# The bound for the softmax: squares kept as a maximum over the blocks, and the shift's rows sent by DMA

## The chip, the cores and the metric

The kernel runs on one core of a Trainium2 chip. The core has a matrix engine (TensorE, PE in the profile, its weight loads PEld), a vector engine (VectorE, DVE), a scalar engine (ScalarE, ACT), GpSimd (POOL), a queue for transfers (SyncE, SP) and 16 DMA engines that all queues share. The metric is the device time of one execution in microseconds (us), lower is better. It is given as the median of several runs, and one more execution is recorded by the profiler.

## The reference

One input x of 2048 tokens with 512 features is normalised. From it come an attention with 32 heads of 16 features and a gated network with 1792 hidden features; the product of the two is added to x.

```python
xn = _layernorm(x)                                    # (1, 2048, 512)
q, k, v = (xn @ wqkv) split into 32 heads of 16
scores = einsum("bhqd,bhkd->bhqk", q, k) * 16 ** -0.5
o = einsum("bhqk,bhkd->bhqd", softmax(scores), v)
s = o.reshape(1, 2048, 512) @ wo
g = silu((silu(xn @ w_gate) * (xn @ w_up)) @ w_down)
return x + s * g
```

All inputs are fp32. The softmax is over all 2048 keys, with no mask.

## The kernel before, in words

The work is written out by hand: each engine runs its instructions in the order in which the code issues them, and waits where its operands are not ready. Products in fp32 are split into a high and a low part (fp32r), so that a projection of one tile takes 12 products: 4 chunks of the 512 features, 3 terms each.

**The first stage** is the pool block `pro` (lines 446 to 797). It goes over 4 blocks of 512 tokens. A block has 12 slots: 8 feature tiles (`feature_tile`, 128 features of queries for m below 4, of keys above) and 4 value tiles (`value_tile`, 128 tokens each). Block 0 does its value tiles first, the others last. While block b is projected, the x of block b + 1 is loaded, its statistics are taken (`stats`, `rates`: L533 to L549), its tiles are normalised (`norm`, L553, VectorE) and transposed on TensorE (`turn_x`, L556), and the transposed tile is split into its high part (ScalarE, L565) and its low part (VectorE, L568). `rates` comes in slot 5, the first `norm` in slot 6, the first transpose in slot 7.

A feature tile is 12 products into a PSUM tile (four of these rotate), then ScalarE writes the squares in bf16 (`sq`, L637) and the high part (L638), VectorE the low part (`parts`, L639), and SP sends both parts to DRAM (L641). GpSimd makes the low parts of the weights (L497) and sends the transposed x and the values to DRAM.

**The shift.** Softmax is taken without a maximum of its own for each query. A common bound serves all queries: half of the largest sum of squares of a query and of a key, times 1.02, which no product of the two passes. For that the squares of each block are summed over the 16 features of a head on TensorE (`squares`, L595, a product with the indicator `ind`), 8 products for each block, put into the two PSUM banks `bankx` and `banky`. `flush` issues them (for block 0 behind the first tile of block 1, for the others in slot 8) and takes the maximum of each bank (L683). Before the last value tiles, the maxima are joined: over partitions by a transpose (`tops`, L745, L746), scaled by 0.51 (L747), and compared with 160 (`flag`, L748). If the flag were 0, the general path in `tc.If` (L765) would find a maximum for each query. The shift goes into the score products as two more rows of the queries (`qst`; the matching rows of `kst` are ones): its high and its low part, the low one 0 here. Two small products (`sel`, `selq`, L754 and L755) put the number on the partitions that need it, ScalarE copies it into `shift` and into the first `qst` (L756, L759), and GpSimd stores `shift` to the DRAM tensor `sh_d` in four parts (L761). From there each later set of queries gets its rows (`load_shift`, L113).

**In slot 9 of the last block** a first hidden feature of the gated network is computed between value tiles (`fill`, L174 for its products; `split_gu` L134 and L135 for its weights, `load_gu` L127 for a later feature's).

**The second stage** goes over 32 units (8 groups of 4 heads, 4 query blocks). Each unit has 8 steps: 8 score products (L835), 4 exponentials on ScalarE (L837), 16 value products (L356), and between them shares of the gated network (`ffn`, L174) by a fixed plan. Its tiles take the SBUF space of the first stage, so some of its first instructions wait until the last transfers of that stage have read their source.

Of the kernel before, what the change touches and what calls it, by code (L numbers as in the profile page):

```python
# [9 lines left out]
F32 = mybir.dt.float32  # L10
F32R = mybir.dt.float32r
BF = mybir.dt.bfloat16
I32 = mybir.dt.int32
AF = mybir.ActivationFunctionType
ALU = mybir.AluOpType
# [35 lines left out]
def tile_block(ctx: ExitStack, tc: tile.TileContext, x, wqkv, wo, w_gate, w_up, w_down, out):  # L51
# [394 lines left out]
    with ExitStack() as pro:  # L446
        pc = pro.enter_context(tc.tile_pool(name="pc", bufs=1))
        p2 = pro.enter_context(tc.tile_pool(name="p2", bufs=2))
        p3 = pro.enter_context(tc.tile_pool(name="p3", bufs=4))
        p5 = pro.enter_context(tc.tile_pool(name="p5", bufs=9))  # L450
        plast = pro.enter_context(tc.tile_pool(name="plast", bufs=1))
        pps = pro.enter_context(tc.tile_pool(name="pps", bufs=4, space=PSUM))

# [55 lines left out]
        dve.memset(ind, 0.0)  # L509
        dve.reduce_sum(indf, ident.rearrange("p (h d) -> p h d", d=DH), axis=AX.X)  # L510
        dve.tensor_copy(ind[:, :8], indf)
        sel = plast.tile([1, 2 * NG * NB], F32, name="sel")
        selq = plast.tile([1, HALF + 2], F32, name="selq")
        row = plast.tile([1, 512], F32, name="row")
        dve.memset(sel, 0.0)
        dve.memset(selq, 0.0)
        dve.memset(row, 1.0)
        peak = pc.tile([P, 2, NB], F32, name="peak")
        vt = plast.tile([P, NG, NT, VW], F32, name="vt")
        vt5 = vt.rearrange("p g t (h d) -> p g t h d", h=4)  # L520
        for t in range(NT):
# [103 lines left out]

        s4 = pc.tile([1, 1], F32, name="s4")
        flag = const.tile([1, 1], I32, name="flag")
        pk = pc.tile([P, 2], F32, name="pk")
        sm = pc.tile([P, 1], F32, name="sm")
        shift = plast.tile([2 * NG * NB, 512], F32R, name="shift")  # L630

        def feature_tile(b, m):
            xh, xl = xt[b % 2]
            ps = project([(wh[:, m, c], wl[:, m, c], c) for c in range(DT)], xh, xl, None)
            parts = p3.tile([P, 2, TB], F32R, tag="parts", name="parts")
            sq = p5.tile([P, TB], BF, tag="sq", name="sq")
            act(sq, ps, AF.Square)  # L637
            nc.scalar.copy(parts[:, 0], ps)  # L638
            dve.tensor_sub(parts[:, 1], ps, parts[:, 0].bitcast(F32))  # L639
            dst = (q_d if m < 4 else k_d)[:, (m % 4) * P:(m % 4 + 1) * P, b * TB:(b + 1) * TB]  # L640
            sp.dma_start(dst.rearrange("s f t -> f s t"), parts.bitcast(F32))  # L641
            return m, sq

        def value_tile(b, t):
            xh, xl = xt[b % 2]
# [21 lines left out]
        def copy_fx(i):  # L667
# [2 lines left out]
            j, h = divmod(i, 2)  # L670
            dst = fx[halves[h], j].rearrange("p (c u) t -> u p c t", u=2)[u]
            nc.scalar.copy(dst[:, 2 * w:2 * w + 2], xt[0][j][halves[u], 2 * w:2 * w + 2])

        pend = []

        def add():
            while pend:
                squares(*pend.pop(0))

        def flush(b):  # L680
            add()
            for j in range(2):
                dve.reduce_max(peak[:, j, b:b + 1], banks[j], axis=AX.X)  # L683

        for b in range(NB):
            more = b + 1 < NB
# [2 lines left out]
            for n, (make, i) in enumerate(slots):  # L689
                if b == 0:  # L690
                    if n + 5 < 12:
                        load_w(worder[n + 5])
                    if n >= 2 and n + 2 < 12:
                        high_w(worder[n + 2])
                        low_w(worder[n + 2])
                if n == (1 if b else 2) and more:
                    load_x(b + 1)
                if b == 2 and n in (6, 7):
                    load_gu(n - 6)
                if b == 2 and n == 8:  # L700
                    load_wd(0)
                if not more and n == 2:
                    split_gu(0)
                    for bank in acc:
                        dve.memset(bank, 0.0)
                if not more and n in (1, 3):
                    load_k(0, n // 2)
                if not more and n == 5:
                    load_q(0)
                if not more and n == 6:  # L710
                    for c in range(2):
                        load_v(0, c)
                if b == 0 and n == 1:
                    norm(2)
                    norm(3)
                made = make(b, i)
                if b == 0 and n == 2:
                    split_x(0, 0, xf)
                if b < 2 and 0 <= 12 * b + n - 3 < 16:
                    copy_fx(12 * b + n - 3)  # L720
                if n == 0 and b == 1:
                    flush(0)
                if make is feature_tile:
                    pend.append(made)
                if b == 0 and n == 11:
                    ring(0, 2, one)
                    queries(0, one)
                if more:
                    for t in range(NT):
                        if n == 2 + (t if b else t // 2):  # L730
                            stats(t)
                    if n == (5 if b else 4):
                        rates(0, NT)
                    if 6 <= n < 10:
                        norm(n - 6)
                    if 7 <= n < 11:
                        turn_x(b + 1, n - 7)
                if n == 8 and b:
                    flush(b)
                if not more and n == 8:  # L740
                    dve.reduce_max(pk, peak, axis=AX.X)
                    dve.tensor_add(sm, pk[:, 0:1], pk[:, 1:2])
                if not more and n == 9:
                    tops = pps.tile([P, 512], F32, tag="ps", name="tops")
                    nc.tensor.transpose(tops[0:1, :P], sm, ident)  # L745
                    dve.reduce_max(s4, tops[0:1, :P], axis=AX.X)  # L746
                    dve.tensor_scalar(s4, s4, 0.51, None, op0=ALU.mult)  # L747
                    dve.tensor_scalar(flag, s4, LIMIT, None, op0=ALU.is_le)  # L748
                    dve.tensor_scalar(sel[:, :NG * NB], row[:, :NG * NB], s4, None, op0=ALU.mult)
                    for h in range(2):  # L750
                        dve.tensor_copy(selq[:, h * HALF:h * HALF + 1], s4)
                    fill(3 * DC)
                    low, high = [pps.tile([P, 512], F32, tag="ps", name="low") for _ in range(2)]
                    mm(high[:2 * NG * NB, :8], sel, row[:, :8], start=True, stop=True, skip_group_check=True)  # L754
                    mm(low[:HALF + 2, :8], selq, row[:, :8], start=True, stop=True, skip_group_check=True)  # L755
                    act(shift, high[:2 * NG * NB, 0:1].to_broadcast([2 * NG * NB, 512]), AF.Copy, scale=-1.0)  # L756
                    for h in range(2):
                        two_rows = slice(h * HALF, h * HALF + 2)
                        act(qst[0][two_rows], low[two_rows, None, 0:1].to_broadcast([2, 2, 512]), AF.Copy, scale=-1.0)  # L759
                    for j in range(4):  # L760
                        pool.dma_start(sh_d[:, j * 512:(j + 1) * 512], shift.bitcast(F32))  # L761
                    fast = nc.values_load(flag, min_val=0, max_val=1)


# [177 lines left out]
```

## Time and profile before

| | us |
|---|---|
| median of 3 runs | 1436.54 |
| lowest and highest | 1436.37, 1437.82 |
| profiled execution | 1437.19 |
| its span | 1435.4 |

| engine | busy us | share of the span |
|---|---|---|
| TensorE | 1428.2 | 99% |
| ScalarE | 1112.2 | 77% |
| VectorE | 535.0 | 37% |
| GpSimd | 89.6 | 6% |

In the profile's rows `out<-in` names the tiles of the program, L12 is a line of the kernel, and x is how many instructions are in the row. In a timeline the first column is the start in us, the second the duration, and a bracket gives the idle time in front and what ended it. Products are pipelined, so the distance between two starts tells what one costs in sequence, and its duration doesn't. Rows of groups end with the busy time, the mean of one in ns, and the idle time of the engine in front of them.

The first stage lasts until about 161 us of the span, when the first score is computed.

### The profile page before, as it was taken

Reading aid. Unit: us, or ns where it says so; the run is one execution under the profiler, and the core shown is the slowest. Engines: PE = TensorE matmul, PEld = TensorE weight load, DVE = VectorE, ACT = ScalarE, POOL = GpSimd, SP = SyncE. Lnnn points to the kernel's source line nnn. Section 1 sums busy time; section 2 is a strip of 40 time slices with the busy share of each in tenths; the row PEclk is TensorE's granted clock in tenths of the full one; section 3 lists DMA queues with packets and bytes.
Section 4 is the critical chain, followed back from the end, with each engine's and each line's share of the span. In section 5 each row is a group of like instructions: output and inputs, shape, how many; then the busy total and the mean of one; then the engine's idle time right before and its main releaser. Section 6 shows DMA issues by size and latency. Waiting matters only on the chain.

```text
span 1435.4 us, 26786 instructions
## 1 busy us (share of the span) xinstructions
PE 1428.2 (99%) x11221; PEld 803.6 (56%) x11221; DVE 535.0 (37%) x886; ACT 1112.2 (77%) x1236; POOL 89.6 (6%) x103
## 2 busy tenths in 40 slices
PE   9999999999999999999999999999999999999998
PEld 7778655555555555555555555555555555555555
DVE  5543344112523342134323431243344422243665
ACT  6733688888888888788888888888888887888764
POOL 4200200000000000000000000000000000000154
PEclk9999999999999999999999999999999999999999
DMA  7778652032274321142553320342824210412552
GB/s 222 264 242 253 157 119 64 17 96 60 64 153 119 97 65 34 38 105 71 111 134 90 94 49 12 79 104 58 177 79 121 65 42 12 101 30 78 196 183 104
DMA packets 127668, 149.15 MB, mean 104 GB/s; under 512 B 12604, under 2 KB 79676, under 8 KB 126772
## 3 DMA queue, kind: packets, MB, share of 16 engines
q1 hardware_dynamic: 122196, 126.71, 34.5%
q0 software_dynamic: 4912, 20.12, 3.8%
q8 instruction: 91, 1.49, 0.5%
q10 hardware_dynamic: 432, 0.52, 0.1%
q14 instruction: 37, 0.30, 0.1%
HBM read 107.20 MB, written 40.11 MB: 103 GB/s over the span
## 4 chain that ended last, share of the span: by engine, by line
PE 88%; DVE 0%; issue 0%; DVEq 0%
PE acc L356 33%; PE bankx L174 32%; PE score L835 20%; PE banky L174 3%; DVE y L889 0%; PE acc L882 0%; DVE y L895 0%; PE score L882 0%; PE banky L882 0%; DVEq L938 0%; DVE rl L886 0%; DVEq L895 0%
## 5 line engine op out<-in xcount | busy, mean ns | idle before, releaser
L837 ACT ACTIVATE pr<-score 128x1024 f32<-128x1024 f32 x1024 | 993.2, 1023 | 223.0 <-PE score L835 222.4
L356 PE MATMUL acc<-pr,vst 128*17 128x512 f32 x4096 | 489.2, 595 | 0.0
L835 PE MATMUL score<-qst,kst 50*128 50x512 f32 x2048 | 352.1, 421 | 0.0
L835 PEld LDWEIGHTS score<-qst,kst 50*128 50x128 f32 x2048 | 177.1, 184 | 263.7 <-ACT pr L837 225.7
L174 PE MATMUL bankx<-fx,guh 64*128 64x512 f32 x896 | 288.8, 392 | 0.1
L174 PE MATMUL banky<-fx,guh 64*128 64x512 f32 x896 | 288.8, 392 | 0.0
L356 PEld LDWEIGHTS acc<-pr,vst 128*17 128x17 f32 x4096 | 94.0, 96 | 234.6 <-issue 233.8
L204 DVE SCALAR_TENSOR_TENSOR ga<-th,bankx 128x512 f32<-128x512 f32 x56 | 38.5, 688 | 445.3 <-ACT th L203 445.3
L174 PEld LDWEIGHTS bankx<-fx,guh 64*128 64x128 f32 x896 | 165.7, 185 | 34.5 <-issue 0.9
L174 PE MATMUL banky<-fx,gul 64*128 64x512 f32 x448 | 175.3, 391 | 0.0
L174 PE MATMUL bankx<-fx,gul 64*128 64x512 f32 x448 | 175.3, 391 | 0.0
L174 PEld LDWEIGHTS banky<-fx,guh 64*128 64x128 f32 x896 | 165.7, 185 | 2.8
L174 PE MATMUL banky<-wd,hh 64*128 64x512 f32 x672 | 166.7, 389 | 0.0
L174 PE MATMUL bankx<-wd,hh 64*128 64x512 f32 x672 | 166.6, 389 | 0.0
L174 PEld LDWEIGHTS bankx<-wd,hh 64*128 64x128 f32 x672 | 124.0, 185 | 26.1
L174 PEld LDWEIGHTS banky<-wd,hh 64*128 64x128 f32 x672 | 124.0, 185 | 1.4
L174 PEld LDWEIGHTS bankx<-fx,gul 64*128 64x128 f32 x448 | 82.9, 185 | 17.8
L174 PEld LDWEIGHTS banky<-fx,gul 64*128 64x128 f32 x448 | 82.8, 185 | 1.4
L588 PE MATMUL ps<-xt,wh 128*128 128x512 f32 x256 | 80.9, 397 | 0.1
L222 DVE COPY facc<-bankx 128x512 f32<-128x512 f32 x16 | 11.1, 692 | 171.1 <-PE banky L174 150.3
L135 DVE TENSOR_TENSOR gul<-gur,guh 128x1024 fp32r<-128x1024 f32 x56 | 68.6, 1225 | 2.1
L588 PEld LDWEIGHTS ps<-xt,wh 128*128 128x128 f32 x256 | 47.8, 188 | 11.8 <-DVE xt L568 0.5
(161 smaller groups left out, 1019.1 us busy)
## 6 DMA issues: line engine op xcount, KB each, us to landing
gur<-in_B_w_gate_dram SPq DMA_DIRECT2D x56, 256.0 KB
gur<-in_B_w_up_dram SPq DMA_DIRECT2D x56, 256.0 KB
wdr<-in_B_w_down_dram SPq DMA_DIRECT2D x56, 256.0 KB
kst<-k_d SPq DMA_DIRECT2D x192, 64.0 KB
qst<-q_d SPq DMA_DIRECT2D x192, 64.0 KB
fx<-xt_d SPq DMA_DIRECT2D x24, 512.0 KB
q_d<-parts SPq DMA_DIRECT2D x16, 512.0 KB
k_d<-parts SPq DMA_DIRECT2D x16, 512.0 KB
```

What stands on the lines that cost most here:

```text
L135: dve.tensor_sub(lo, raw, hi.bitcast(F32))
L174: mm(bank, lhs[h], rhs[h], start=start, stop=stop)
L204: dve.scalar_tensor_tensor(ga, th, 1.0, bankx, op0=ALU.add, op1=ALU.mult)
L222: dve.tensor_copy(facc[:, t], bankx)
L356: mm(a[h * 32:h * 32 + DH + 1], v[:, kt % CT, h * (DH + 1):(h + 1) * (DH + 1)], probs[2 * i + h // 2][:, h % 2], start=kt == 0, stop=kt == ...
L588: mm(ps, w, a[:, c], start=n == 0, stop=n == 3 * DT - 1)
L835: mm(score[j][:, h], k[r, j, kc * P:(kc + 1) * P], q[r, j], start=True, stop=True)
L837: exps.append(act(pr, score[j], AF.Exp, scale=0.25))
```

## The change

Squares of block 0 are written straight into eight tiles `top`, one for each feature tile. In the later blocks they go into one of two rotating `sq` tiles (nine before), and VectorE takes the maximum of `top` and `sq` into `top`. The sums over the features of a head are made once, of the eight `top` tiles, in slot 8 of the last block; the two maxima over the banks are taken there, and added. The bound is thereby that of the largest squares at the same place in a block, not of one token; on the reference's inputs it rises from 69 to 99 by its formula.

The shift's row is made on one partition by VectorE (0 plus the number, times -1, 512 columns). SP copies it into the first row of each half of `qst`, and GpSimd stores it to the upper half of `sh_d`, which is read as 128 rows of 512, by one DMA whose source is that one row each time. The rows of the low part, which are 0, are no longer sent with it: GpSimd writes the lower half of `sh_d` at the start from a row of zeros, and clears the two rows in each half of `qst` at the end of block 0. The products L754 and L755, the tiles `sel`, `selq` and `pk`, and the three ScalarE copies are gone.

```diff
-        p5 = pro.enter_context(tc.tile_pool(name="p5", bufs=9))
+        p5 = pro.enter_context(tc.tile_pool(name="p5", bufs=2))
...
-        sel = plast.tile([1, 2 * NG * NB], F32, name="sel")
-        selq = plast.tile([1, HALF + 2], F32, name="selq")
         row = plast.tile([1, 512], F32, name="row")
-        dve.memset(sel, 0.0)
-        dve.memset(selq, 0.0)
-        dve.memset(row, 1.0)
-        peak = pc.tile([P, 2, NB], F32, name="peak")
+        dve.memset(row, 0.0)
+        peak = pc.tile([P, 2], F32, name="peak")
+        top = [pc.tile([P, TB], BF, name=f"top{m}") for m in range(8)]
...
-        shift = plast.tile([2 * NG * NB, 512], F32R, name="shift")
+        shift = plast.tile([1, 512], F32R, name="shift")
+        none = sh_d[NG * NB:].rearrange("u (j t) -> (u j) t", t=512)
+        pool.dma_start(none, row[:, None].to_broadcast([1, NG * NB * 4, 512]))
...
-            sq = p5.tile([P, TB], BF, tag="sq", name="sq")
+            sq = p5.tile([P, TB], BF, tag="sq", name="sq") if b else top[m]
...
-            return m, sq
+            if b:
+                dve.tensor_max(top[m], top[m], sq)
...
-        def flush(b):
-            add()
-            for j in range(2):
-                dve.reduce_max(peak[:, j, b:b + 1], banks[j], axis=AX.X)
...
+                if not more and n == 8:
+
+                    for m in range(8):
+                        squares(m, top[m])
+                    for j in range(2):
+                        dve.reduce_max(peak[:, j:j + 1], banks[j], axis=AX.X)
+                    dve.tensor_add(sm, peak[:, 0:1], peak[:, 1:2])
...
-                if n == 0 and b == 1:
-                    flush(0)
-                if make is feature_tile:
-                    pend.append(made)
                 if b == 0 and n == 11:
                     ring(0, 2, one)
                     queries(0, one)
+                    for h in range(2):
+                        pool.memset(qst[0][h * HALF:h * HALF + 2].bitcast(F32), 0.0)
...
-                    dve.tensor_scalar(sel[:, :NG * NB], row[:, :NG * NB], s4, None, op0=ALU.mult)
+                    dve.tensor_scalar(shift, row, s4, -1.0, op0=ALU.add, op1=ALU.mult)
                     for h in range(2):
-                        dve.tensor_copy(selq[:, h * HALF:h * HALF + 1], s4)
+                        sp.dma_start(qst[0][h * HALF:h * HALF + 1].bitcast(F32), shift.bitcast(F32)[:, None].to_broadcast([1, 2, 512]))
+                    pool.dma_start(sh_d[:NG * NB].rearrange("u (j t) -> (u j) t", t=512),
+                                   shift.bitcast(F32)[:, None].to_broadcast([1, NG * NB * 4, 512]))
                     fill(3 * DC)
-                    low, high = [pps.tile([P, 512], F32, tag="ps", name="low") for _ in range(2)]
-                    mm(high[:2 * NG * NB, :8], sel, row[:, :8], start=True, stop=True, skip_group_check=True)
-                    mm(low[:HALF + 2, :8], selq, row[:, :8], start=True, stop=True, skip_group_check=True)
-                    act(shift, high[:2 * NG * NB, 0:1].to_broadcast([2 * NG * NB, 512]), AF.Copy, scale=-1.0)
-                    for h in range(2):
-                        two_rows = slice(h * HALF, h * HALF + 2)
-                        act(qst[0][two_rows], low[two_rows, None, 0:1].to_broadcast([2, 2, 512]), AF.Copy, scale=-1.0)
-                    for j in range(4):
-                        pool.dma_start(sh_d[:, j * 512:(j + 1) * 512], shift.bitcast(F32))
```

More of the change, by code (lines that the diff above doesn't have):

```diff
@@ L627, in tile_block @@
         flag = const.tile([1, 1], I32, name="flag")
-        pk = pc.tile([P, 2], F32, name="pk")
         sm = pc.tile([P, 1], F32, name="sm")
-        shift = plast.tile([2 * NG * NB, 512], F32R, name="shift")
+        shift = plast.tile([1, 512], F32R, name="shift")
+        none = sh_d[NG * NB:].rearrange("u (j t) -> (u j) t", t=512)
+        pool.dma_start(none, row[:, None].to_broadcast([1, NG * NB * 4, 512]))
         def feature_tile(b, m):
@@ L672, in copy_fx @@
             nc.scalar.copy(dst[:, 2 * w:2 * w + 2], xt[0][j][halves[u], 2 * w:2 * w + 2])
[L674 to L678, printed above, removed]
-        def flush(b):
-            add()
-            for j in range(2):
-                dve.reduce_max(peak[:, j, b:b + 1], banks[j], axis=AX.X)
         for b in range(NB):
@@ L737, in tile_block @@
                         turn_x(b + 1, n - 7)
[L738 to L742, printed above, removed]
                 if not more and n == 9:
```

## The prediction

> **What bounds the kernel now.** I read the page's first two parts, then TensorE's busy time by stretch, then the timelines of TensorE, VectorE and the queues around the lines that the change touches. The page comes first.
>
> ```profile
> span 1435.4 us, 26786 instructions
> PE 1428.2 (99%) x11221; PEld 803.6 (56%) x11221; DVE 535.0 (37%) x886; ACT 1112.2 (77%) x1236; POOL 89.6 (6%) x103
> PE   9999999999999999999999999999999999999998
> ```
>
> TensorE has work in flight for 99% of the span. The same holds in the first 160 us, the stage that the change edits (columns: span, then each engine's busy us and its instructions, granted clock, DMA share, GB/s):
>
> ```profile
> 100.00:140.00 40.00, 40.00 (x187) 32.05 (x186) 16.62 (x32) 15.24 (x29) 1.99 (x3) 1.00 0.83 251
> 140.00:160.00 20.00, 20.00 (x117) 15.04 (x115) 7.02 (x16) 7.11 (x10) 2.11 (x4) 1.00 0.66 173
> ```
>
> The clock granted is 1.00 and TensorE is never idle, so in this stage a product taken off its queue is worth its whole place there, and a wait put before a product costs its whole length. VectorE is busy 42% (16.62 of 40 us) and GpSimd 5%. Nothing after about 162 us is edited: that stage moves earlier or later as a block.
>
> **Part 1: three of four groups of sums go.** Before, each of the four blocks is followed by 8 products of L595; after, only the last is. The groups on TensorE's timeline (start, us, engine, line; x is how many were merged), the first three in order:
>
> ```profile
> 49.10 0.40 PE L588 MATMUL ps<-xt,wl 128*128 128x512 f32 x1
> 49.42 0.40 PE L595 MATMUL bankx<-sq,ind 128*32 128x512 bf16 x4
> 49.65 0.39 PE L595 MATMUL banky<-sq,ind 128*32 128x512 bf16 x4
> 49.97 0.73 PE L588 MATMUL ps<-xt,wh 128*128 128x512 f32 x2
> ...
> 72.82 0.60 PE L556 MATMUL acc<-ident,xn 128*128 128x128 f32 x4
> 73.89 0.73 PE L590 MATMUL ps<-vh,xt 128*128 128x512 f32 x2
> 76.78 0.60 PE L556 MATMUL acc<-ident,xn 128*128 128x128 f32 x4
> 77.13 0.71 PE L590 MATMUL ps<-vh,xt 128*128 128x512 f32 x2
> ...
> 108.78 0.60 PE L556 MATMUL acc<-ident,xn 128*128 128x128 f32 x4
> 109.85 0.73 PE L590 MATMUL ps<-vh,xt 128*128 128x512 f32 x2
> ```
>
> Four sums run side by side (0.23 us for four), so a group is cheap. From the product before it to the one behind it the first group takes 49.97 - 49.10 = 0.87 us. Two neighbouring products without a group are 0.23 us apart (the four products of 49.42 and those of 49.65 show the same pitch), so it costs 0.64. The second and third stand behind four transposes: 73.89 - 72.82 = 1.07 and 109.85 - 108.78 = 1.07, against 77.13 - 76.78 = 0.35 for four transposes with no group behind them, so 0.72 each. Gain: 0.64 + 0.72 + 0.72 = 2.08 us.
>
> **Part 2: the two products of the shift go.**
>
> ```profile
> 153.52 0.39 PE L174 MATMUL banky<-fx,gul 64*128 64x512 f32 x1
> 153.84 0.28 PE L754 MATMUL low<-row,sel 1*64 1x8 f32 x2
> 154.26 0.50 PE L590 MATMUL ps<-vh,xt 128*128 128x512 f32 x1
> ```
>
> From the last hidden-layer product to the next projection it is 0.74 us. Without L754 and L755 the switch from half-height to full-height products stays; the switch to L754 shows it as 0.32. Gain 0.42 us; at most 0.51, if the plain pitch of 0.23 came back. On ScalarE the three copies of the shift (L756, L759) go as well, and on VectorE six of eight reductions (L683): neither engine sets the end there, so both count as nothing. Both parts together: 2.50 us.
>
> **Part 3: 24 maxima on VectorE.** Each stands right behind the subtraction of its tile (L639), in blocks 1 to 3. Their cost shows in no row. These kinds of operation bound it (mean ns of one, then idle time in front):
>
> ```profile
> L135 DVE TENSOR_TENSOR gul<-gur,guh 128x1024 fp32r<-128x1024 f32 x56 | 68.6, 1225 | 2.1
> L134 DVE CAST guh<-gur 128x1024 fp32r<-128x1024 f32 x56 | 38.4, 686 | 0.0
> L166 DVE CAST hh<-ga 128x512 fp32r<-128x512 f32 x56 | 23.9, 428 | 12.5 <-ACT pr L837 10.6
> L639 DVE TENSOR_TENSOR parts<-ps,parts 128x512 fp32r<-128x512 f32 x32 | 22.1, 690 | 50.0 <-ACT parts L638 50.0
> ```
>
> An operation with two inputs costs 690 ns for 512 columns of four bytes and 1225 for 1024: about 155 fixed and 1.04 a column. A cast goes at half of that (428 and 686). The maximum has two inputs, which speaks for 690, but of two bytes: in words of four bytes it has 256 columns, 155 + 256 x 1.04 = 0.42 us. I take 0.43, as the cast's row has it, and keep 0.69 as the other end. The Trainium skill, page VectorE: DVE Perf Modes, section The perf-mode tier table, lets a two-tensor operation on 16-bit data in SBUF go at two results a cycle, and at one on fp32. By that rule the sum below is the one with 0.43; by the plain two-input row it is the one with 0.69.
>
> 24 x 0.43 = 10.3 us is less than the 50.0 us that VectorE idles in front of the 32 subtractions, so most of it is hidden. One place has no cover, the chain to the first normalised tile of the next block (VectorE and the weight load, PEld):
>
> ```profile
> 65.32 0.69 DVE L639 TENSOR_TENSOR parts<-ps,parts 128x512 fp32r<-128x512 f32 x1 [1.28 <-ACT parts L638]
> 65.93 0.68 DVE L533 BATCH_NORM_STATS2 st<-facc 128x6 f32<-128x512 f32 x1
> 67.19 0.18 DVE L545 RECIPROCAL rs<-nw 128x4 f32<-128x4 f32 x1 [0.16 <-ACT nw L542]
> 68.34 0.69 DVE L639 TENSOR_TENSOR parts<-ps,parts 128x512 fp32r<-128x512 f32 x1
> 68.94 0.54 DVE L553 TENSOR_SCALAR xn<-facc,mv,rs 128x512 f32<-128x512 f32 x1
> 69.53 0.42 PEld L556 LDWEIGHTS acc<-ident,xn 128*128 128x128 f32 x4 [0.22 <-DVE xn L553]
> 69.59 0.60 PE L556 MATMUL acc<-ident,xn 128*128 128x128 f32 x4
> ...
> 105.50 0.42 PEld L556 LDWEIGHTS acc<-ident,xn 128*128 128x128 f32 x4 [0.22 <-DVE xn L553]
> ```
>
> From 65.32 to 69.48 VectorE runs without a pause except 0.16 us: subtraction, statistics, rates, subtraction, normalisation. TensorE's transpose (L556) needs that normalised tile, and its weight load already waits 0.22 us for it: the slack is used up to the last 0.06 us, in block 1 and again in block 2. After the change two maxima (tiles 5 and 6) stand inside this chain. An operation of 0.69 lets the next start 0.61 later (65.32 to 65.93), so one of 0.43 moves it by 0.35. The transposes start 2 x 0.35 = 0.70 us late, and all of TensorE's queue behind them too. Two blocks: 1.40 us lost. Tile 4's maximum fits in the 1.28 us of idle time at 65.32, and in the later transposes VectorE has more slack than that. At 0.69 it would be 4 x 0.61 = 2.44 us; if something in the chain gave way, 0.
>
> The last sums read the maxima instead of the squares. The subtraction of tile 7 and TensorE's second four of the group:
>
> ```profile
> 142.81 0.69 DVE L639 TENSOR_TENSOR parts<-ps,parts 128x512 fp32r<-128x512 f32 x1 [2.09 <-ACT parts L638]
> 144.62 0.39 PE L595 MATMUL banky<-sq,ind 128*32 128x512 bf16 x4
> ```
>
> The last maximum ends at about 142.81 + 0.61 + 0.43 = 143.85, or 144.1 at 0.69, before 144.62. No cost. The two buffers of sq in place of nine let ScalarE run two tiles (5.6 us) ahead of VectorE, and it is never that far ahead. The looser bound (69 before, 99 after on these inputs, by its formula) stays under the limit of 160, so the general path isn't taken.
>
> **Part 4: transfers in place of products.** The rows on SP, VectorE and PEld, the old stores of the shift, the queue's use of the DMA engines in 155.3 to 160.5 us, and the two places early on where a new clearing store falls:
>
> ```profile
> 145.19 1.32 SPq L127 DMA_DIRECT2D gur<-in_B_w_up_dram  x1
> 148.71 0.22 DVE L749 TENSOR_SCALAR sel<-row,s 1x32 f32<-1x32 f32 x1
> 161.02 0.46 PEld L835 LDWEIGHTS score<-qst,kst 50*128 50x128 f32 x4
> 169.15 0.80 DVE L134 CAST guh<-gur 128x1024 fp32r<-128x1024 f32 x1
> ...
> DMA to landing us min/median/max: 2.4/3.6/3.9
> ...
> q0 software_dynamic: 192, 0.52, 41.8%
> ...
> 18.35 1.30 POOL L497 TENSOR_TENSOR wl<-wraw,wh 128x512 fp32r<-128x512 f32 x1 [5.30 <-ACT wh L493]
> 26.19 0.69 DVE L639 TENSOR_TENSOR parts<-ps,parts 128x512 fp32r<-128x512 f32 x1 [1.65 <-ACT parts L638]
> ```
>
> The shift's row is one VectorE operation of 512 columns in place of three small ones: ready at 148.71 + 0.54 = 149.25. SP then sends two copies to qst, the second at about 149.7; with the old stores' longest landing, 3.9 us, they are there at 153.6. The first score loads weights at 161.02 - 0.42 = 160.6: 7.0 us of slack. SP now waits for that row, and behind it are the two weight loads that went out by 145.19: they leave at about 150 to 152 and are used at 169.15. GpSimd sends 256 KB in one store in place of 512 KB in four, 6 us earlier. The clearing store falls into GpSimd's idle 5.30 us before 18.35, and the two clears of qst rows come behind its last work of block 0. Nothing of this lies on the path: 0.
>
> How long a 256 KB transfer read from a single row takes, T, shows in no row. Low end: the old stores kept 41.8% of the engines for 5.2 us over 0.52 MB, so half of it is 1.1 us. High end: each of their 64 rows gave 8 KB in those 2.2 us, so one row alone would need 32 x 2.2 = 70 us. I take the low end, because the pieces are of the same 2 KB; the other is rival B.
>
> **Sum.** -2.08 - 0.42 + 1.40 = -1.10 us. The profiled execution took 1437.19 us (span 1435.4 and 1.8 around it); it lies 0.65 above the median of three, 1436.54. After: 1436.1 for such an execution, **1435.4 for the median**, 0.08% less.
>
> **The rivals.**
> - A, VectorE hides its maxima: the statistics of tile 5 move or the chain gives way, and the 1.40 us do not come. Time 1436.54 - 2.50 = 1434.0. Against it: the 0.22 us wait of both rows.
> - C, the maximum costs 0.69: the stall is 2.44 us and takes back the gain, 1436.5. For it: the two-input rows.
> - B, slower: the single-row store holds the DMA engines. It starts near 150.3, and the second copy to qst, issued at about the same time, could be behind it; it lands at 150.3 + T + 2.4 and is late from T = 7.9. Each further us is lost once at the first score: no gain is left from T = 9.0, and the loss passes 0.2% from T = 11.9. With T = 18 the time is 1435.4 + 10.1 = 1445.5. The clearing store at 13 us would hold loads for statistics and weights in the same way; there 1.65 us of VectorE's idle time at 26.19 and more later cover a few us. Against it: 7 us of slack and old stores that cost little.
> - The Trainium skill, page SBUF — State Buffer, section Door 1: The DMA port swizzle, says that four neighbouring partitions share one port and measured 27.6 GB/s for partitions 0 to 3. By that rule T would be 9.5 us, an estimate from the page: 0.5 us slower than before if the second copy is behind the store. No run here shows such a read yet.
>
> **How the numbers follow.** My forecast (stall between 1.0 and 1.8) 40%, A and values between 17%, C 15%, B past 0.2% 12%, B below it 4%, things that I don't see 12%, of which 7 on the fast side and 5 on the slow one. What a measurement of this kernel can tell from no change is about 0.2%, 2.9 us. A, C and my forecast all lie within it, and so does B while T is below 11.9. Faster by more needs something unseen, since only 2.50 us are removed: 7%. Slower by more: 12 + 5 = 17%. Within it: 76%. The forecast's own range is 1434.8 to 1436.0. The 80% range reaches from a little below A to B with T near 11: 1433.4 to 1438.6.
>
> **What would show it.** Eight products with ind instead of 32, and projections 0.23 us apart where the first group was: part 1. A gap in TensorE of about 0.7 us in front of the transposes near 69 and 105 us, released by VectorE's xn: part 3; the maximum's mean ns decides between my forecast and C. The first score near 160 us with no wait for a DMA: part 4; a wait there, or loads that land late after 13 us, is B. The attention stage as long as before: if it isn't, the prediction is wrong at a place that I hold untouched.

## The result, and the profile after

The changed kernel takes 1445.05 us, the median of 5 runs (1444.26 to 1445.58), against 1436.54 us before (1436.32 to 1437.82): a ratio of 1.0057, 95% interval 1.0045 to 1.0068. It is slower by 8.5 us, where 1.1 us less was forecast; 1445.05 lies outside the range of 1433.4 to 1438.6. The profiled execution also took 1445.05 us, with a span 7.4 us longer than before. The page's first line and its line of TensorE's slices, then the stretches around the place of the change (columns as in the prediction):

```profile
span 1442.8 us, 26740 instructions
PE   9999899999999999999999999999999999999998
...
156.00:159.00 3.00, 0.00 (x0) 0.00 (x0) 0.02 (x1) 0.00 (x0) 0.00 (x0) 0.79 0.92 29
159.00:162.00 3.00, 2.79 (x7) 2.25 (x8) 0.00 (x0) 0.00 (x0) 0.00 (x0) 0.50 0.54 129
162.00:165.00 3.00, 3.00 (x10) 2.33 (x9) 0.00 (x0) 0.30 (x1) 0.00 (x0) 0.58 0.27 64
```

The page alone hides the loss: of TensorE's slices only the fifth has fallen, from 9 to 8. The stretches show it. TensorE does nothing from 156 to 159 us, and then runs on half its clock (0.50) until about 164.5. While it stands the DMA engines are almost fully taken (a share of 0.92) and move only 29 GB/s. Now the timelines of TensorE, GpSimd and SP, the landing time of the two stores to sh_d, and the queues' use of the engines in 149.5 to 160 us:

```profile
153.49 0.39 PE L174 MATMUL banky<-fx,gul 64*128 64x512 f32 x1
159.21 1.19 PE L587 MATMUL ps<-vh,xt 128*128 128x512 f32 x2 [5.32 <-issue]
160.20 0.63 PE L587 MATMUL ps<-vl,xt 128*128 128x512 f32 x1
...
168.62 0.64 PE L816 MATMUL score<-qst,kst 50*128 50x512 f32 x4
...
149.45 0.54 POOL L740 DMA_DIRECT2D sh_d<-shift  x1 [28.28 <-DVE shift L737]
149.22 1.46 SPq L739 DMA_DIRECT2D qst<-shift  x2
150.73 6.88 SPq L127 DMA_DIRECT2D gur<-in_B_w_gate_dram  x1
...
DMA to landing us min/median/max: 11.5/11.5/11.6
...
q0 software_dynamic: 69, 0.26, 82.9%
q1 hardware_dynamic: 36, 0.02, 2.1%
```

The fill ends in both kernels at the same time (153.49 here; 153.52 before). Then TensorE stands for 5.32 us, "issue": the profile has nothing that it waits for. In the program one instruction of TensorE lies between the fill and L587, the register load of the flag (L743). In just that time GpSimd's store of 256 KB from a single row (L740) is under way, from 149.45 to its landing 11.6 us later, on q0, which keeps 82.9% of the 16 engines. SP's issue of a weight load is held for 6.88 us. From 153.49 to 159.21 it is 5.72 us against 0.74 before: 5.0 lost. The 24 products behind it take 8.4 us in place of 6.0, by the clock: 2.4 more. Together 7.4, the whole difference of the spans. The profile shows no wait before the first score (168.62).

### The profile page after: what moved, and what is told of

It is laid out like the page before. It is cut to its first block, busy times and chain, and to the rows that moved or that the text cites. A ratio compares the mean times of both kernels' runs of the same rounds, so it can differ in the third digit from the quotient of the medians.

```text
span 1442.8 us, 26740 instructions
## 1 busy us (share of the span) xinstructions
PE 1428.6 (99%) x11193; PEld 805.1 (56%) x11193; DVE 539.0 (37%) x899; ACT 1110.0 (77%) x1233; POOL 90.0 (6%) x103
## 4 chain that ended last, share of the span: by engine, by line
PE 88%; DVE 0%; issue 0%; DVEq 0%
PE acc L356 33%; PE bankx L174 31%; PE score L816 20%; PE banky L174 3%; DVE y L870 0%; PE acc L863 0%; DVE y L876 0%; PE score L863 0%; PE banky L863 0%; DVEq L919 0%; DVE rl L867 0%; DVEq L876 0%
## 5 line engine op out<-in xcount | busy, mean ns | idle before, releaser
L356 PE MATMUL acc<-pr,vst 128*17 128x512 f32 x4096 | 489.2, 595 | 0.0
L356 PEld LDWEIGHTS acc<-pr,vst 128*17 128x17 f32 x4096 | 94.0, 97 | 234.1 <-issue 233.4
L585 PEld LDWEIGHTS ps<-xt,wh 128*128 128x128 f32 x256 | 47.9, 188 | 11.5 <-DVE xt L565 0.5
```

The costliest lines, as they stand in the source:

```text
L356: mm(a[h * 32:h * 32 + DH + 1], v[:, kt % CT, h * (DH + 1):(h + 1) * (DH + 1)], probs[2 * i + h // 2][:, h % 2], start=kt == 0, stop=kt == ...
L585: mm(ps, w, a[:, c], start=n == 0, stop=n == 3 * DT - 1)
```

## The experiments

The expectations speak of two theories. **Theory 1**: TensorE's register load of the flag, a read of SBUF, stands behind the one-row store, at the port of that partition (1a) or at engines that the store holds (1b). **Theory 2**: instructions come too late while the store holds the engines. Profiles differ by about 1 us in the first 20 us already (the small transpose of L745 starts at 147.84 us in the kernel before, and at 146.85 in gap_short, which is the same up to there), so where it matters I count from a row nearby rather than from the span. Each ratio is to the kernel before as it was run again beside that version; its medians there were 1436.30 to 1437.38 us.

| kernel | median, us | ratio to before (95%) |
|---|---|---|
| changed | 1445.05 | 1.0057 (1.0045 to 1.0068) |
| flag_first | 1444.49 | 1.0053 (1.0036 to 1.0069) |
| port | 1443.73 | 1.0052 (1.0035 to 1.0069) |
| half | 1438.99 | 1.0014 (1.0004 to 1.0023) |
| zeros128 | 1443.41 | 1.0045 (1.0028 to 1.0062) |
| spread | 1436.41 | 0.9994 (0.9985 to 1.0003) |
| squares_only | 1436.12 | 0.9995 (0.9986 to 1.0004) |
| extra_store | 1443.51 | 1.0047 (1.0034 to 1.0061) |
| late_max | 1435.23 | 0.9987 (0.9978 to 0.9996) |
| flag_late | 1445.20 | 1.0063 (1.0046 to 1.0079) |
| gap_short | 1441.56 | 1.0038 (1.0024 to 1.0052) |
| gap_long | 1443.83 | 1.0056 (1.0039 to 1.0072) |
| no_branch | 1440.32 | 1.0026 (1.0016 to 1.0035) |
| short_path | 1443.14 | 1.0047 (1.0030 to 1.0064) |

**flag_first: the flag is read before the store starts.**

```diff
+                    fast = nc.values_load(flag, min_val=0, max_val=1)
                     dve.tensor_scalar(shift, row, s4, -1.0, op0=ALU.add, op1=ALU.mult)
...
                     fill(3 * DC)
-                    fast = nc.values_load(flag, min_val=0, max_val=1)
```

> One line is moved: the register load of the flag stands ahead of the shift's row, its transfers and the fill. The last profile shows TensorE standing 5.3 us behind the fill (153.85 to 159.2 us) while one store reads 256 KB from a single row of SBUF (149.45, landing 11.5 us), and a slow clock (0.50 to 0.79) for 9 us after. Theory 1 (TensorE's load of the flag, a read of partition 0, waits behind that store's reads): the load is done before the store starts, so the gap behind the fill and the slow clock after it go; in their place TensorE waits about 1 us for the flag ahead of the fill (148.0 to about 149). 1445.05 - 5.3 - 2.4 + 1 = about 1438.3 us, the store itself unchanged. Theory 2 (the instructions after the branch, or those of the value tiles, are fetched too late): the gap stays where the fill ends, about 1445 or 1446 us.

Measured 1444.49: no gain. TensorE's timeline in this kernel (PEq and SPq stand for what TensorE's and SyncE's instruction sequencers did at that line):

```profile
149.79 0.47 PE L174 MATMUL bankx<-fx,guh 64*128 64x512 f32 x1 [1.26 <-DVE flag L736]
...
155.26 0.39 PE L174 MATMUL banky<-fx,gul 64*128 64x512 f32 x1
155.59 0.73 PE L587 MATMUL ps<-vh,xt 128*128 128x512 f32 x2
...
163.97 0.47 PE L174 MATMUL bankx<-fx,guh 64*128 64x512 f32 x1 [2.52 <-PEq L746]
166.18 1.42 PE L816 MATMUL score<-qst,kst 50*128 50x512 f32 x4 [1.01 <-SPq L746]
```

Half of theory 1 came true: the gap behind the fill is gone (155.26 to 155.59), and the 1.26 us wait for the flag stands ahead of the fill. So the gap was the wait for the flag's read. But the time did not come back: TensorE now stops at the branch (L746), 2.52 us and then 1.01, and the slow clock follows there. Taking away one wait showed the next one behind the same store.

**port: the row lies in another partition than the flag.**

```diff
-        row = plast.tile([1, 512], F32, name="row")
+        row = plast.tile([HALF + 1, 512], F32, name="row")[HALF:]
...
-        shift = plast.tile([1, 512], F32R, name="shift")
+        shift = plast.tile([HALF + 1, 512], F32R, name="shift")[HALF:]
```

> The row of the shift lies in partition 64 in place of partition 0 (with the maximum that makes it); the flag stays in partition 0. The store still reads one row, 256 KB. Theory 1a (the flag's read and the store's reads meet at one port of SBUF, that of the neighbouring partitions): no gap behind the fill, full clock, store landing 11.5 us as before; about 1437.3 us. Theory 1b (the flag's read waits because the engines that carry it are taken by the store, whatever partition it reads) or theory 2 (instruction fetch): the gap stays, about 1445 us.

```profile
157.70 1.19 PE L587 MATMUL ps<-vh,xt 128*128 128x512 f32 x2 [3.93 <-issue]
...
DMA to landing us min/median/max: 11.6/11.6/11.6
```

The gap is 3.93 us in place of 5.32, with the slow clock behind it. Theory 1a explains at most those 1.4 us; the store lands as late from partition 64 as from 0, and the read waits all the same.

**half: the store sends half as much.** An added early store from 64 rows keeps the other half of the shift's rows at zeros, so this kernel leaves out the shift in units 16 to 31.

```diff
...
-                    pool.dma_start(sh_d[:NG * NB].rearrange("u (j t) -> (u j) t", t=512),
-                                   shift.bitcast(F32)[:, None].to_broadcast([1, NG * NB * 4, 512]))
+                    pool.dma_start(sh_d[:NG * NB // 2].rearrange("u (j t) -> (u j) t", t=512),
+                                   shift.bitcast(F32)[:, None].to_broadcast([1, NG * NB * 2, 512]))
```

> The late store sends 64 rows (128 KB) in place of 128; the shift's rows of units 16 to 31 stay at the zeros that an added transfer of 128 KB from 64 rows puts there early, so the subtraction of the shift is left out for those units. If the store's time is bytes through one row (256 KB took 11.5 us with about 2.4 us of fixed cost, so 9.1 us of transfer), it lands in about 6.9 us, is over at about 156.5 and the gap behind the fill shrinks from 5.3 to about 1 us; if the slow clock comes from TensorE's idle time it goes with it: about 1438.5 us. If the gap does not depend on the store it stays: 1445 us.

Measured 1438.99, as expected. The first value product and the landing times of the stores to sh_d (6.8 is the late one), then the clock's stretch behind it:

```profile
155.75 0.71 PE L587 MATMUL ps<-vh,xt 128*128 128x512 f32 x2 [1.28 <-ACT th L203]
...
DMA to landing us min/median/max: 6.8/9.2/11.7
...
156.00:159.00 3.00, 3.00 (x14) 2.42 (x14) 0.61 (x1) 0.18 (x1) 0.00 (x0) 1.00 0.67 169
```

The gap shrinks to 1.28 us and the clock stays at 1.00. (The row names ScalarE's `th`, but that had ended at 155.10; the last 0.65 us are again a wait that the profile doesn't show.) The landing grows by 11.6 - 6.8 = 4.8 us for 128 KB more: 27 GB/s through one row, and 9.6 us for 256 KB.

**zeros128: only the early clearing store is spread over 128 rows.**

```diff
-        row = plast.tile([1, 512], F32, name="row")
+        row = plast.tile([P, 512], F32, name="row")
...
-        pool.dma_start(none, row[:, None].to_broadcast([1, NG * NB * 4, 512]))
+        pool.dma_start(none, row)
...
```

> Only the early clearing store is changed: it reads zeros from 128 rows in place of one. It lands in about 3 us in place of 11.5; the load of A's rows that stood behind it comes early again (VectorE's wait for it 3.39 us back to about 0.4). The late store and its gap of 5.3 us stay. If the early store costs nothing at the end, about 1445.0 us; if VectorE's late start is part of the loss, down to 1444.5.

Measured 1443.41; its interval overlaps the changed kernel's, so no gain is shown. The store lands in 2.7 us as expected, but the late load does not follow (VectorE's wait for A's rows):

```profile
59.41 0.69 DVE L530 BATCH_NORM_STATS2 st<-facc 128x6 f32<-128x512 f32 x1 [3.38 <-DMA facc<-in_A_x_dram]
```

The wait is 3.38 us as in the changed kernel (3.39), so the one-row reading of the early store does not cause it. What does stays open: in squares_only (below) it is 0.81, but that kernel leaves out two things, the clearing store and the two clears of `qst` rows, which GpSimd does here from 50.1 to 52.1 us, just when this load is issued (50.5). No run separates them.

**spread: no transfer reads a single row of SBUF many times.** To the edit of zeros128 this adds:

```diff
+                    sp.dma_start(one_d, shift.bitcast(F32))
                     pool.dma_start(sh_d[:NG * NB].rearrange("u (j t) -> (u j) t", t=512),
-                                   shift.bitcast(F32)[:, None].to_broadcast([1, NG * NB * 4, 512]))
+                                   one_d.to_broadcast([NG * NB * 4, 512]))
```

> Both transfers from a single row are spread, all else is the changed kernel: the clearing store reads 128 rows, and the shift's row goes once to DRAM (2 KB, SP's queue) and from there, DRAM to DRAM, 128 times into its place. If the one-row store is the whole loss (theory 1 and 2 alike), the sum without it comes out: -2.08 - 0.42 + 1.34 (the two stalls as measured, 0.84 + 0.50) = -1.2 us against before, about 1435.5 to 1436, no gap behind the fill, clock 1.00. If a DRAM-to-DRAM copy from 2 KB holds the engines as well, the gap comes back in full: +8 us.

Measured 1436.41, 0.9994 of before: the loss is gone. The median is 0.8 us under that of the kernel before (1437.19), near the 1.1 of the forecast's sum, but the interval includes no change. The timelines of TensorE, SP and the landing:

```profile
147.72 0.27 PE L734 MATMUL tops<-ident,sm 128*1 128x128 f32 x1
153.72 0.73 PE L587 MATMUL ps<-vh,xt 128*128 128x512 f32 x2
...
151.09 0.70 SPq L127 DMA_DIRECT2D gur<-in_B_w_gate_dram  x1
...
DMA to landing us min/median/max: 4.9/4.9/4.9
```

From the small transpose to the first value product it is 6.00 us, against 6.42 before (147.84 to 154.26): exactly the 0.42 us of part 2. A store of the same 256 KB, sent from one row in DRAM, lands in 4.9 us, and SP's issue is no longer held (0.70 for 6.88).

**squares_only: the maxima and the one set of sums, the shift by products as before.**

```diff
...
+                    mm(high[:2 * NG * NB, :8], sel, row[:, :8], start=True, stop=True, skip_group_check=True)
+                    mm(low[:HALF + 2, :8], selq, row[:, :8], start=True, stop=True, skip_group_check=True)
...
+                    for j in range(4):
+                        pool.dma_start(sh_d[:, j * 512:(j + 1) * 512], shift.bitcast(F32))
```

> The maxima and the one set of sums of the changed kernel, with the shift by products and four stores of 64 rows as before. Expected: -2.08 + 1.34 = -0.7 us against before, no gap behind the fill. If VectorE's maxima had a part in the loss of 8 us, it shows here.

Measured 1436.12, 0.9995: the maxima have no part in the 8 us. Its first transposes of block 1 wait 0.51 us for VectorE's xn, where the changed kernel's wait 0.84 (below).

**extra_store: the kernel before plus one store.**

```diff
...
                         dve.tensor_copy(selq[:, h * HALF:h * HALF + 1], s4)
+                    dve.tensor_scalar(row, row, s4, None, op0=ALU.min)
+                    pool.dma_start(extra, row[:, None].to_broadcast([1, P, 512]))
```

> The kernel before with one thing added at the place where the changed one sends the shift: a VectorE operation that makes a row of 512 (ones, which the products read as before), and a store of that row, 128 times, 256 KB, to a place in DRAM that nothing reads. Theory 1 and 2 (the one-row store alone makes the loss): the gap before the value tiles (here behind the two small products) of about 5 us and the slow clock, landing 11.5 us: +7 to +8 us against before, about 1444.5. If the loss needs something else of the change (the flag's read with no products before it, the copies to qst), about 0 to +1 us.

```profile
158.37 1.19 PE L591 MATMUL ps<-vh,xt 128*128 128x512 f32 x2 [5.18 <-issue]
```

A store whose bytes nothing reads costs 1443.51 - 1437.19 = 6.3 us (6.8 by the ratio), and the gap of 5.18 us stands in front of the value tiles, though SP sends nothing there. TensorE goes on 9.77 us after the store was issued (148.60), in the changed kernel 9.76 us after (149.45 to 159.21): in both about the 9.6 us that half gave for 256 KB. One such store is enough to make the loss.

**late_max: spread, with the stalls of part 3 taken out.** The maxima of tiles 5 and 6 in blocks 1 and 2 go behind the next block's first normalisation.

```diff
-            if b:
+            if b and (m in (5, 6) and b < NB - 1):
+                pend.append((m, sq))
+            elif b:
                 dve.tensor_max(top[m], top[m], sq)
...
+                    while n == 6 and pend:
+                        m, sq = pend.pop(0)
+                        dve.tensor_max(top[m], top[m], sq)
```

> As spread, and the maxima of tiles 5 and 6 in blocks 1 and 2 stand behind the first normalisation of the next block in place of ahead of it. If the stalls ahead of the transposes (0.84 and 0.50 us) are those two maxima, they go: 1.3 us less than spread, -2.5 us against before, about 1434. If VectorE was late for another reason (the statistics behind a late load), the stalls stay: as spread.

Measured 1435.23, 0.9987 (0.9978 to 0.9996): the only version here whose interval lies under the kernel before, by 2.0 us in the medians. That is 1.2 us less than spread, where 1.3 was expected. TensorE's busy time in the two stretches of the stalls, in the changed kernel and then in this one:

```profile
60.00:80.00 20.00, 19.16 (x90) 15.33 (x89) 13.09 (x32) 11.50 (x19) 0.00 (x0) 1.00 0.59 203
100.00:120.00 20.00, 19.50 (x93) 15.71 (x92) 9.93 (x25) 7.80 (x15) 1.07 (x2) 1.00 0.75 220
```

```profile
60.00:80.00 20.00, 19.88 (x94) 16.00 (x94) 13.29 (x33) 11.02 (x19) 0.53 (x1) 1.00 0.51 174
100.00:120.00 20.00, 20.00 (x96) 16.18 (x95) 8.68 (x22) 7.32 (x15) 1.99 (x3) 1.00 0.79 239
```

**flag_late: the flag is read right in front of the branch**, behind the value tiles.

```diff
-                    fast = nc.values_load(flag, min_val=0, max_val=1)
...
+        fast = nc.values_load(flag, min_val=0, max_val=1)
         with tc.If(fast < 1):
```

> The changed kernel with the register load of the flag moved behind the two value tiles, right in front of the branch that uses it; nothing else. The one-row store stays and lands 11.5 us after 149.5, at 161. Theory 1 (TensorE's gap is the flag's read standing behind the store): TensorE goes on with the value tiles at 153.9, comes to the read at about 160, where the store is nearly over; what is left is 0 to 1 us, no slow clock: 1436 to 1437 us. Theory 2 (instructions come too late while the store holds the engines; the stops at the branch of 2.5 and 1.0 us with the flag read early speak for it): stops of 2 to 4 us behind the branch at 160 to 165, where a slow clock follows: 1440 to 1443 us.

```profile
154.04 0.73 PE L587 MATMUL ps<-vh,xt 128*128 128x512 f32 x2
...
159.51 0.40 PE L587 MATMUL acc<-vl,xt 128*128 128x512 f32 x1
164.69 0.76 PE L174 MATMUL bankx<-fx,guh 64*128 64x512 f32 x1 [4.78 <-PEq L746]
```

The value tiles run without a gap, which shows once more that the gap came with the read. Then TensorE stands 4.78 us at the branch, on after the store has landed (at 161.3), with the slow clock behind it: 1445.20. Moving the read only moves the loss.

**gap_short and gap_long: TensorE idle, with no transfer.** One or six VectorE operations hold the small products of the kernel before.

```diff
                     fill(3 * DC)
+                    for _ in range(6):
+                        dve.tensor_scalar(row, row, s4, None, op0=ALU.min)
                     low, high = [pps.tile([P, 512], F32, tag="ps", name="low") for _ in range(2)]
```

> The kernel before, with TensorE held behind the fill by VectorE alone: one more operation on the row of ones that the two small products read, placed behind the fill's last VectorE operations. No transfer is added. TensorE stands from 153.9 to about 156.6, 2.7 us. If the slow clock follows idle time only from about 3.4 us on, the loss is that gap: +2.5 to +2.8 us against before, clock 1.00. If shorter gaps do it too, a stretch at 0.50 follows and it is +4 to +6.

> As gap_short with six such operations: TensorE stands from 153.9 to about 159.2, 5.3 us, as long as in the changed kernel, with no transfer added. If TensorE's idle time makes the slow clock: a stretch at 0.50 of some 6.8 us that begins inside the gap, +5.3 and about +2.4, together +7 to +8 us, about 1444. If the store makes it: +5.3 us and the clock at 1.00.

The gap and the stretches behind it, of gap_short and then of gap_long:

```profile
155.59 0.25 PE L756 MATMUL low<-row,sel 1*64 1x8 f32 x2 [2.67 <-DVE row L754]
...
156.00:159.00 3.00, 2.89 (x9) 2.31 (x9) 0.00 (x0) 2.38 (x3) 2.10 (x4) 0.62 0.37 81
159.00:162.00 3.00, 3.00 (x12) 2.36 (x12) 0.00 (x0) 0.59 (x1) 0.00 (x0) 0.81 0.41 111
```

```profile
158.18 0.35 PE L756 MATMUL low<-row,sel 1*64 1x8 f32 x2 [5.21 <-DVE row L754]
...
156.00:159.00 3.00, 0.82 (x5) 0.80 (x6) 1.90 (x4) 0.43 (x1) 0.00 (x0) 0.62 0.00 0
159.00:162.00 3.00, 3.00 (x8) 2.33 (x9) 0.00 (x0) 2.07 (x3) 2.10 (x4) 0.50 0.44 96
162.00:165.00 3.00, 3.00 (x12) 2.40 (x11) 0.00 (x0) 0.59 (x1) 0.00 (x0) 0.75 0.36 90
```

The idle time alone makes the slow clock. Between 1.00 and 0.50 a mean of 0.62 over 3 us means 2.3 us of slow clock, 0.81 means 1.1: 3.4 us in gap_short. In gap_long it is 2.3 + 3.0 + 1.5 = 6.8, in the changed kernel 1.3 + 3.0 + 2.5 = 6.8. Gap and clock together cost 5.3 and 7.5 us by the medians.

**no_branch: flag and branch unused.** The register load and the whole general path are taken out, so this kernel has no answer for inputs whose bound is over 160.

> The changed kernel without the branch: the flag is computed but no engine reads it, and the general path behind the branch (for inputs whose bound is over the limit) is left out. The one-row store stays. If the loss is in the two waits that the flag brings (TensorE's read of it, and the branch at which TensorE stood until 164.0 and 164.7 us when the read was moved), TensorE runs from the fill through the value tiles into the first scores at about 160.2 without a stop, clock 1.00: about -1 us against before, 1435.5. If instructions as such come too late behind the store, or if the first score waits for qst's second copy, TensorE stops at 160 to 164 us all the same and the clock drops: +4 to +8 us.

```profile
159.98 0.40 PE L587 MATMUL acc<-vl,xt 128*128 128x512 f32 x1
160.31 0.49 PE L174 MATMUL bankx<-fx,guh 64*128 64x512 f32 x1
...
161.98 0.70 PE L783 MATMUL score<-qst,kst 50*128 50x512 f32 x3 [0.26 <-DMA qst<-shift]
...
162.00:165.00 3.00, 3.00 (x23) 2.25 (x25) 0.00 (x0) 2.47 (x3) 0.00 (x0) 1.00 0.95 266
```

1440.32, between the two expectations. Value tiles, branch place and clock are as theory 1 said, and 4.7 us of the loss are gone. What is left, 3.8 us against before, shows in part. The first score does wait for the second copy to qst, as rival B had it: from its first product to the next of the hidden layer it is 0.98 us (161.34 to 162.32) against 0.46 in spread (160.73 to 161.19), so 0.5 us lost, of which the row counts 0.26 as idle. The first value products of the attention (L356) start 0.8 us later than in the kernel before (166.79 for 166.03), the third set 1.6 us later (177.38 for 175.74), after a wait for VectorE's `ga` (L205) near 175 us. The rest isn't explained; these runs spread more than others (1438.92 to 1442.05).

**short_path: flag_late with the general path's loops cut to one turn each.**

```diff
-                for g in range(NG):
-                    for b in range(NB):
+                for g in range(1):
+                    for b in range(1):
...
-                            for i in range(4 * NT):
+                            for i in range(1):
```

> The kernel with the flag's read moved in front of the branch, and the loops of the general path cut to one turn each (some 160 of TensorE's and VectorE's instructions fewer between the branch and its target; the general path, which these inputs don't take, would no longer compute its result). If the stop of 4.8 us at the branch comes from instructions that must be fetched past the long path: it goes or shrinks to under 1 us, no slow clock, 1438 to 1441 us as without the branch. If an engine is late at the branch for its own read of the flag or for SyncE's held weight load: the stop stays, 1444 to 1445.5 us.

```profile
159.72 0.47 PE L174 MATMUL bankx<-fx,guh 64*128 64x512 f32 x1 [0.85 <-PEq L746]
163.64 1.46 PE L816 MATMUL score<-qst,kst 50*128 50x512 f32 x4 [2.72 <-SPq L746]
...
163.55 0.38 SPq L778 DMA_DIRECT2D v_d<-vt  x1
```

The stop at the branch shrinks from 4.78 to 0.85 us, so most of it came from the length of the path that is jumped over. That fits theory 2, as do the instruction queues: in the kernel before q8 and q14 bring packets in 149.5 to 160 us, in the changed one none do (its two queues above are all there are):

```profile
q0 software_dynamic: 192, 0.52, 20.7%
q1 hardware_dynamic: 461, 0.22, 11.7%
q14 instruction: 4, 0.03, 1.2%
q8 instruction: 2, 0.03, 1.1%
```

The times of these packets tell the two waits apart. In the changed kernel the first come after 162.0 us, and TensorE had gone on at 159.21: its gap did not end by instructions arriving. In flag_late q14 brings some from 161.5 to 163 us and again between 164.5 and 165, and TensorE leaves the branch at 164.69. Which packet belongs to which engine isn't shown.

But the time stays at 1443.14, since a third wait comes up: the first score waits 2.72 us for SP, which leaves the branch only at about 163.5. Its weight loads were issued by 159.2 us, so it isn't late for them; in no_branch it goes on 0.4 us after them. Whether it was its own read of the flag or its instructions isn't told apart: on q8 and q14 no packet came between 159.5 and 166.5 us.

## Why the prediction was wrong

The step that failed is part 4, "Nothing of this lies on the path: 0". Three things were wrong in it; the first two make the loss.

- **The size of T.** I took the low end, 1.1 us, "because the pieces are of the same 2 KB". Measured, the store goes at 27 GB/s (half): T is 9.6 us. The prediction's sentence on the Trainium skill, page SBUF — State Buffer, section Door 1: The DMA port swizzle, had it right: 27.6 GB/s, 9.5 us. What counts is how many rows are read, not the size of the pieces: the early store of the same 2 KB pieces landed in 11.5 us from one row and in 2.7 from 128 (zeros128).
- **Who is late.** Even with 9.6 us rival B would have forecast a loss of about 0.6, since I looked for the victim among the transfers that the score waits for. That one costs 0.5 us where it shows (no_branch). The real ones are not transfers in the program's lists: TensorE's register load of the flag (L743), 5.0 us, then the clock that falls in the gap, 2.4 us, and hidden behind them the branch (4.78 us in flag_late) and SP (2.72 in short_path). The slack of 7 us that I named belonged to the wrong reader; the flag's read had none. Rival B's figure of 1445.5 with T = 18 is near the result by accident.
- **SP's weight loads** were to leave "at about 150 to 152". The first one's issue was held until 157.6.

The other steps hold. **Part 1**: products where the first group stood are 0.24 us apart (49.49 to 49.73), and four transposes with none behind them take 0.36 (73.53 to 73.89), so 0.63 and 0.71 for the 0.64 and 0.72 forecast. **Part 2**: 0.42 as forecast (spread). **Part 3**: the maxima and the two stalls in the changed kernel are

```profile
L641 DVE TENSOR_TENSOR top<-top,sq 128x512 bf16<-128x512 bf16 x24 | 10.0, 415 | 0.0
...
70.25 0.66 PE L553 MATMUL acc<-ident,xn 128*128 128x128 f32 x4 [0.84 <-DVE xn L550]
106.20 0.66 PE L553 MATMUL acc<-ident,xn 128*128 128x128 f32 x4 [0.50 <-DVE xn L550]
```

415 ns for the forecast 430, which rules out rival C. The idle times, 0.84 and 0.50 us, are not the whole of the stalls. From the product in front to the transposes it is 1.24 us (69.01 to 70.25) and 0.90 (105.30 to 106.20) where the kernel before has 0.24 (69.35 to 69.59): 1.00 and 0.66 lost, 1.66 for the forecast 1.40. Block 2 is near the forecast 0.70. Block 1 stalls longer, as VectorE also waits 3.39 us for A's rows there; in squares_only, where that wait is 0.81, both blocks lose about 0.65. That the stalls are there rules out rival A; late_max shows that they can be avoided. With part 4 repaired the sum fits: -2.05 - 0.42 + 1.66 = -0.8 by the measured terms, and spread is 0.8 us under its kernel before (1436.41 against 1437.19), where 1.1 was forecast; the interval alone would not show so small a gain. The attention stage is untouched, as forecast: the span's difference of 7.4 is all there at the first score (168.62 for 161.25).

## What to carry to other kernels

A transfer that reads one row of SBUF many times goes at the rate of one row (27 GB/s here) and can hold nearly all DMA engines meanwhile (a share of 0.92 here); keep it away from branches and register loads, or make the copies from a row in DRAM or from many rows. When such a hold is suspected, list everything that fetches through memory in that stretch: the profile shows a register load's wait only as "issue", and when one wait is moved, the next stands behind the same cause. A gap of TensorE can cost more than its length: the clock fell in or behind the gaps of 2.5 us and more, and the products that then ran on half the clock took twice their time. The gap of 1.28 us cost no clock.

## What was unexpected of the hardware

- TensorE's register load from SBUF waited 5.3 us behind one store, with the store's row in the same partition, and 3.9 us with it in partition 64: TensorE went on 9.8 us after the store was issued, or 8.2 (149.47 to 157.70). What it queues for isn't settled.
- TensorE's clock fell to 0.50 after 2.67 us of idle time (gap_short), but not after 1.28 (half), and stayed there for 3.4 us or twice that. In port it had fallen already some 2.0 us after the last product (153.77; the mean of 0.96 in 153 to 156 us puts the fall at about 155.8). The Trainium skill, page TensorE: Matmul & The Clock Gate, Part 1, has a free-running window of 3.4 us and a halved clock after an idle window; the two lengths of the slow stretch agree. It asks for about 3.4 us of idle time, and here a gap of 2.67 us was enough, and in port about 2.0 us of idle time.
- 256 KB sent from one row in DRAM landed in 4.9 us, from one row in SBUF in 11.6 us.
